# Two units' value bounds from sums of magnitudes on ScalarE instead of maxima on VectorE, with a new order of steps

## The chip, the cores and the metric

The kernel runs on one core of a Trainium2 chip. The metric is the device time of one execution in microseconds; the median of several runs is compared. Engines are named as in the profile: PE (TensorE, matmuls), PEld (TensorE's weight loads), DVE (VectorE), ACT (ScalarE), POOL (GpSimd), SP (SyncE, which issues the DMAs).

## The reference

Banded attention over 8 heads feeds a two-layer network. Heads 0 to 3 see the last 32 keys, heads 4 to 7 every fourth key of the last 128.

```python
def _attn_ref(q, k, v):                       # (8, 8, 576, 64)
    scores = scale * np.matmul(q, k.transpose(0, 1, 3, 2))
    scores = np.where(masks[None, :, :, :], scores, -1000000000.0)
    scores = scores - np.max(scores, axis=-1, keepdims=True)
    attn = np.exp(scores)
    attn = attn / (np.sum(attn, axis=-1, keepdims=True) + 1e-09)
    return np.matmul(attn, v)

def _moe_ref(x, w_in, w_out):                 # (4608, 512), (512, 2048), (2048, 512)
    h = x @ w_in
    sp = np.where(h > 20.0, h, np.log1p(np.exp(np.minimum(h, 20.0))))
    g = h * np.tanh(sp)
    return g @ w_out
```

## The kernel before

The work is cut into 16 units of 288 tokens (half of a batch entry each), numbered from 0. A unit's attention runs head by head; its output x is split into a high and a low float16 word, and so are the weights, so that each product of the network is three float16 matmuls.

The first four units are *direct*: their scores are float32 matmuls on the loaded q and k. Units from 4 on split q, k and v into words as well. The weights arrive as 64-bit numbers, 1 MB at a time, in four raw buffers, and are turned into words by VectorE, ScalarE and GpSimd during the first 180 us. This preparation shares the first units' time with their attention.

Every scale by which a split is made is a power of two taken from a bound on the values. For a direct unit `prep(u)` (line 477) takes that bound from v alone: `amax` (line 309) reduces the magnitudes of `vn` (128 partitions of 768 numbers) and `vdn` (72 or 104 partitions of 1024) to a maximum per partition on VectorE, one operation takes the greater of the two, `over_partitions` (line 317) carries it over the partitions with a transpose and a matmul on TensorE, and `pow2_scales` makes the scale `f`. With it `values` forms the divisor `den`, and `ff_scales` the factors of the network.

The order of all this is written out. `ORDER` (line 37) is a list of step names, and a loop at the end calls each step up to its next `yield` whenever its name comes up; each engine works through its instructions in the order that this leaves. A name's parts are numbers of unit, head, pair, weight matrix or column block:

- `ld`, `lv` load q and k, or v; `pr` is `prep`; `sp` a pair of heads' scores, `sc` the maxima of a head's scores, `ex` its exponentials, `tp` their transpose, `va` the products with v, `tx` the transpose of x and its split.
- `wl`, `wm`, `ws`, `ww`, `wp` load, scan, scale and split weights: matrix 0 or 1 (w_in, w_out), column block, half. `wp0.3.0` is the split of the first half of block 3 of w_in.
- `ff` is one of 16 column tiles of the first product (line 860, 12 matmuls) with its activation on ScalarE (line 865) out of one of four PSUM banks; `gt` the split of four activated tiles; `fo` the second product (line 911) and its output.
- `ol` (`open_late`, line 696) gives the raw buffers' space to new buffers and fills those with zeros on GpSimd; `mr` makes a mask.
- `kwN` gives N matmuls of zeros by zeros into an unused place (`keep_warm`, line 937): they stand where TensorE would have nothing to do.

SP issues the DMAs in this order too: a load into a raw buffer waits until the split of the weights that were in it is done, and the loads behind it wait with it.

Of the kernel before, what the change touches and what calls it, by code (L numbers as in the profile page):

```python
# [42 lines left out]
ws0.0 va0.7 tp0.4 fs0.3 wm0.2.0 tp0.5 ws0.0 tx0.0 kw2 va0.4 tx0.0 ww0.0.0 tp0.5 kw9 tx0.0 tx0.0 kw2 sp0.1 wp0.0.1
va0.5 ld1 sc0.2 va0.5 va0.4 va0.4 kw15 ex0.2 sc0.3 ex0.2 fs0.0 wm0.1.0 kw11 ex0.3 va0.5 tp0.2 wp0.0.1 ex0.3 tp0.2 kw14
tp0.3 tx0.3 pr1 tp0.3 wl0.2.1 kw2 va0.2 tx0.3 va0.3 tx0.2 lv2 va0.2 kw2 tx0.3 va0.3 tx0.2 va0.2 ww0.1.0 tx0.3 va0.3
ww0.2.0 kw16 kw16 kw2 tx0.1 tx0.2 ww0.1.0 tx0.1 tx0.2 kw11 tx0.1 kw2 sp1.0 tx0.1 wp0.0.0 ff0.12 sc1.0 sc1.1 ex1.0
sp1.1 wp0.0.0 ex1.1 ff0.15 sc1.3 wm0.2.1 wl0.1.1 ld2 ff0.14 sc1.2 ex1.3 ff0.12 ww0.2.1 tp1.0 tp1.1 ww0.2.0 ff0.13
# [5 lines left out]
ff0.8 tx1.1 fs0.1 va1.5 tp1.6 tx1.1 ff0.4 va1.5 tp1.7 tx1.1 tp1.6 ff0.11 pr2 va1.6 ff0.10 tx1.2 va1.7 tx1.2 ff0.7
va1.7 va1.6 ff0.9 va1.6 tx1.2 wm1.3.1 pr2 ff0.5 va1.7 pr2 tx1.2 tx1.3 ww1.3.0 ff0.4 ff0.6 tx1.3 ww1.3.1 gt0.0 gt0.2
pr2 tx1.3 pr2 sp2.0 ff0.5 ws1.3 ff0.6 sc2.1 tx1.3 sc2.0 ff0.7 gt0.2 ff1.8 ex2.1 ws1.3 ff1.11 ex2.0 ww1.3.1 ff1.0 gt0.1
tp2.0 sp2.1 tp2.0 fs1 ff1.10 gt0.1 ld3 ff1.8 lv3 ww1.3.0 sp2.3 ff1.0 ff1.2 ff1.11 ff1.10 wm1.1.0 sc2.2 ff1.9 wp1.3.0
ww1.1.0 ff1.4 sc2.3 ff1.2 wp1.3.0 ff1.9 ff1.6 ff1.4 wm1.1.1 ww1.1.0 wl1.2.1 ff1.1 ff1.6 ex2.2 ff1.3 sc2.7 sc2.6
fo0.3.0 wp1.3.1 ww1.1.1 ww1.1.1 ws1.1 ex2.3 wp1.3.1 ex2.6 fo0.3.1 ws1.1 wl1.2.0 gt1.2 sp3.2 wp1.1.0 gt1.2 ff1.5 sc3.4
sc3.5 gt1.2 tp2.1 fo0.3.2 fs2 tp2.1 ex3.4 va2.0 wp1.1.1 fo0.3.3 ff1.1 wp1.1.1 sp3.1 va2.0 ff1.5 ff1.12 sc3.3 wp1.1.0
ff1.3 fo0.3.3 va2.0 ff1.14 wp1.1.1 pr3 wl1.0.1 ff1.12 wp1.1.1 tp2.2 ff1.14 va2.1 ff1.7 wm1.2.0 sc3.2 wm1.2.1 ww1.2.0  # L60
ff1.13 wl1.0.0 tp2.2 ww1.2.1 tp2.3 ff1.15 ww1.2.1 tp2.3 gt1.0 va2.2 fo0.1.0 ff1.7 ww1.2.0 va2.2 gt1.1 ws1.2 gt1.0
ff1.15 ff1.13 va2.1 gt1.1 wm1.0.1 fo0.1.1 va2.1 va2.2 gt1.3 ws1.2 va2.3 fo0.1.2 wm1.0.0 gt1.3 sp3.0 va2.3 ex2.7
ww1.0.1 gt1.1 fo1.3.0 sc3.0 va2.3 tx2.0 fo1.1.0 tx2.0 wp1.2.0 tp2.6 sc3.1 wp1.2.0 fo1.3.1 tp2.6 ex3.5 tx2.0 tp2.7
va2.6 gt1.3 tp2.7 sp2.2 va2.6 wp1.2.0 tx2.1 sc2.4 ld4 fo1.3.2 ex3.0 sc2.5 wp1.2.0 tx2.1 va2.6 ex2.4 fo0.1.3 fo0.3.3
va2.7 fo1.3.3 va2.7 ex2.5 va2.7 ww1.0.1 fo1.1.1 ww1.0.0 tx2.1 tp2.5 tx2.1 fo0.2.0 tp2.5 pr4 tp2.4 tx2.3 ws1.0 ww1.0.0
tx2.3 tp2.4 fo0.1.3 wp1.2.1 va2.4 ws1.0 fo0.1.3 fo1.2.0 ex3.2 va2.4 tx2.3 va2.5 fo1.1.2 va2.5 va2.4 pr4 fo0.2.1
wp1.0.0 wp1.2.1 tp3.4 pr3 tp3.4 fo1.1.3 va2.5 tp3.5 wp1.0.1 tx2.2 tp3.5 fo1.2.1 fo1.3.3 pr3 wp1.0.1 ex3.3 fo1.3.3
# [148 lines left out]
@with_exitstack
def attn_mish_ffn_kernel(
# [91 lines left out]
    def amax(o, i, axes=None):  # L309
        axes = axes or {2: AX.X, 3: AX.XY, 4: AX.XYZ}[len(i.shape)]  # L310
        nc.vector.tensor_reduce(o, i, axis=axes, op=ALU.max, apply_absolute_value=True)
# [684 lines left out]
```

## Time and profile before

| | us |
|---|---|
| median of 3 runs | 926.02 (925.3 to 926.18) |
| the profiled execution | 926.27 |
| its span, first to last instruction | 924.2 |

The page gives each engine's busy time and its share of the span. A row of instructions reads: line, engine, operation, output<-input, count, then busy time and mean duration, then the idle time of the engine just ahead of it and what ended that. A row of a timeline begins with the start and the duration in us. A row of waits reads: engine and line that waited, what it waited for, total us, how often, the longest. A row of windows reads: stretch, its length, busy time and count, granted clock as a share, busy share of the DMA engines, GB/s.

### The profile page before, as it was taken

Reading aid. Unit: us, or ns where it says so; the run is one execution under the profiler, and the core shown is the slowest. Engines: PE = TensorE matmul, PEld = TensorE weight load, DVE = VectorE, ACT = ScalarE, POOL = GpSimd, SP = SyncE. Lnnn points to the kernel's source line nnn. Section 1 sums busy time; section 2 is a strip of 40 time slices with the busy share of each in tenths; the row PEclk is TensorE's granted clock in tenths of the full one; section 3 lists DMA queues with packets and bytes.
Section 4 is the critical chain, followed back from the end, with each engine's and each line's share of the span. In section 5 each row is a group of like instructions: output and inputs, shape, how many; then the busy total and the mean of one; then the engine's idle time right before and its main releaser. Section 6 shows DMA issues by size and latency. Waiting matters only on the chain.

```text
span 924.2 us, 22677 instructions
## 1 busy us (share of the span) xinstructions
PE 913.6 (99%) x9431; PEld 738.4 (80%) x9431; DVE 647.2 (70%) x1344; ACT 551.7 (60%) x1058; POOL 57.1 (6%) x116
## 2 busy tenths in 40 slices
PE   9999999999999999999999999999999999999998
PEld 8878778787778787878788788878787887887876
DVE  4998988677774786879888777887874775624120
ACT  3688784567465657577576565747555673635241
POOL 1002143501000000000000000000000000000000
PEclk9999999999999999999999999999999999999999
DMA  7846532130523425253726242333314221221200
GB/s 245 234 145 209 142 111 66 59 102 2 127 55 75 73 77 114 57 141 42 167 50 144 40 120 56 100 91 93 92 34 112 72 55 34 55 55 25 70 1 26
DMA packets 158102, 82.42 MB, mean 89 GB/s; under 512 B 124496, under 2 KB 153904, under 8 KB 158000
## 3 DMA queue, kind: packets, MB, share of 16 engines
q1 hardware_dynamic: 158000, 80.97, 35.1%
q8 instruction: 74, 1.21, 0.6%
q14 instruction: 28, 0.23, 0.1%
HBM read 49.02 MB, written 9.44 MB: 63 GB/s over the span
## 4 chain that ended last, share of the span: by engine, by line
PE 97%; DMA 1%; ACT 1%; DVE 1%; issue 0%; ACTq 0%; SPq 0%
PE f L860 41%; PE f L911 40%; PE psc L619 4%; PE pav L761 3%; PE f L939 3%; PE pav L755 2%; PE ptp L734 1%; PE psc L668 1%; PE psc L616 1%; DMA g<-p 0%; DMA pT<-p 0%; PE pm L369 0%; PE px L804 0%; PE pm L372 0%; DVE fo L917 0%; PE px L817 0%
## 5 line engine op out<-in xcount | busy, mean ns | idle before, releaser
L860 PE MATMUL f<-x,w 128*128 128x288 f16 x3072 | 393.6, 286 | 1.6 <-ACT hm L865 1.6
L911 PE MATMUL f<-g,w 128*128 128x288 f16 x3072 | 389.9, 286 | 0.0
L860 PEld LDWEIGHTS <-w 128*128 128x128 f16 x3072 | 294.7, 98 | 76.1 <-issue 1.7
L911 PEld LDWEIGHTS <-w 128*128 128x128 f16 x3072 | 296.4, 98 | 73.6
L865 ACT ACTIVATE hm<-f,fs 128x288 f32<-128x288 f32 x256 | 121.3, 497 | 120.9 <-PE f L860 120.2
L901 DVE SCALAR_TENSOR_TENSOR g<-hm,sg,g 128x1152 f16<-128x1152 f32 x59 | 82.9, 1411 | 55.9 <-ACT g L899 55.8
L923 ACT ACTIVATE y<-f,fo 128x288 f32<-128x288 f32 x60 | 41.8, 717 | 82.5 <-PE f L911 68.5
L899 ACT ACTIVATE g<-hm,sg 128x1152 f16<-128x1152 f32 x59 | 73.6, 1252 | 0.6
L776 DVE RECIPROCAL rec<-den 72x4 f32<-72x4 f32 (+1 forms) x128 | 21.4, 167 | 68.6 <-ACT den L772 59.9
L653 DVE TENSOR_TENSOR sb<-sb,nm 96x256 f32<-96x256 f32 (+4 forms) x120 | 55.5, 462 | 4.1
L778 DVE TENSOR_TENSOR xs<-pav,rec 72x256 f32<-72x256 f32 (+1 forms) x128 | 49.6, 387 | 11.0 <-DVE rec L776 0.5
L651 DVE TENSOR_REDUCE nm<-sb 96x2 f32<-96x256 f32 (+4 forms) x120 | 53.7, 448 | 3.3
L687 ACT ACTIVATE sb<-sb,ln_p 96x352 f32<-96x352 f32 (+3 forms) x96 | 52.8, 585 | 0.1
L772 ACT ACTIVATE den<-pav 96x3 f32<-96x3 f32 (+1 forms) x96 | 15.0, 165 | 58.7 <-PE pav L761 58.4
L645 DVE SCALAR_TENSOR_TENSOR sb<-psc,sc,m_s 72x288 f32<-72x288 f32 (+1 forms) x48 | 27.6, 575 | 27.3 <-PE psc L619 27.2
L725 DVE TENSOR_TENSOR p<-sb,p 96x352 f16<-96x352 f32 (+3 forms) x57 | 29.3, 523 | 22.1 <-ACT p L723 22.1
L534 ACT ACTIVATE q<-qn,s 128x144 f16<-128x144 f32 (+1 forms) x60 | 30.6, 590 | 10.3 <-DVE s L307 7.6
L793 ACT CAST g<-xs 96x384 f16<-96x384 f32 (+1 forms) x48 | 26.7, 562 | 14.8 <-DVE xs L778 13.1
L645 DVE SCALAR_TENSOR_TENSOR sb<-psc,sc,m_r 96x352 f32<-96x352 f32 (+1 forms) x48 | 28.4, 592 | 9.7 <-PE psc L619 9.7
L939 PE MATMUL f<-zeros 128*128 128x128 f16 x491 | 33.6, 227 | 1.0 <-DVE zeros L935 1.0
L619 PEld LDWEIGHTS <-q 64*72 64x72 f16 (+1 forms) x1008 | 26.4, 115 | 10.3 <-issue 9.5
L619 PE MATMUL psc<-k,q 64*96 64x128 f16 (+3 forms) x1008 | 32.7, 210 | 0.0
(140 smaller groups left out, 921.0 us busy)
## 6 DMA issues: line engine op xcount, KB each, us to landing
qn<-in_qT SPq DMA_DIRECT2D x16, 576.0 KB
out_T<-y SPq DMA_DIRECT2D x64, 144.0 KB
raw<-in_w_in SPq DMA_DIRECT2D x16, 512.0 KB
raw<-in_w_out SPq DMA_DIRECT2D x16, 512.0 KB
vn<-in_v SPq DMA_DIRECT2D x48, 128.0 KB
vdn<-in_vd SPq DMA_DIRECT2D x32, 104.0 KB
knd<-in_kdT SPq DMA_DIRECT2D x16, 208.0 KB
knp<-in_kT SPq DMA_DIRECT2D x8, 320.0 KB
```

The lines of the kernel that those rows point to most:

```text
L619: nc.tensor.matmul(o, q, k, start=start, stop=stop, skip_group_check=True)
L645: nc.vector.scalar_tensor_tensor(shaped(sb), shaped(pt), d["sc"][:nq], mask, ALU.mult, ALU.add)
L651: nc.vector.tensor_reduce(nm[:nq, j:j + n], x, axis=AX.X, op=ALU.max, negate=True)
L653: nc.vector.tensor_tensor(o, x, nm[:nq, j:j + n].unsqueeze(2).broadcast_to([nq, n, w]), op=ALU.add)
L687: nc.scalar.activation(x, x, AF.Exp, bias=ln_p[:nq])
L778: nc.vector.tensor_tensor(xs[:nq, :nb, (head % 2) * D:(head % 2 + 1) * D], avv[:, :, :D], rc.unsqueeze(2).broadcast_to([nq, nb, D]), op=AL ...
L860: nc.tensor.matmul(ph[:, :HT], w1[j][:, c, wi, k * P:(k + 1) * P], x_of(d, xi, c), start=(n == 0), stop=(n == len(seq) - 1))
L865: nc.scalar.activation(d["m"][j][:, k], ph[:, :HT], AF.Mish, scale=d["fs"][:, j:j + 1])
L899: nc.scalar.activation(g[:, 0], m, AF.Identity, scale=sg)
L901: nc.vector.scalar_tensor_tensor(g[:, 1], m, sg, g[:, 0], ALU.mult, ALU.subtract)
L911: nc.tensor.matmul(po[:, :HT], w2[:, e, j, wi, k * P:(k + 1) * P], d["g"][j][:, gi, k, :], start=(j == 0 and n == 0), stop=(j == NCH - 1 a ...
L939: nc.tensor.matmul(fbs[3][:, 512 - P:], zeros, zeros, start=True, stop=True)
```

## The change

For units 0 and 1 (`SUMMED`) the bound is no longer the greatest magnitude of a partition but the sum of its magnitudes, which is never less. ScalarE makes it: two passes with the function Abs, whose results are added up into `m` as they go by. The passes' own output is bfloat16 and is thrown away; it goes to the last block of `w2`, which is written with weights later. The greater of the two is then taken on VectorE as before, after a new `yield`, so `pr0` and `pr1` come up once more in the list. The list itself is new from its 39th step on.

```diff
@@ ORDER, 2682 steps before and 2690 now
-kw16 ... sp0.0 wp0.3.0 sp0.3 sc0.0 sc0.1 wp0.3.1 ex0.0 sc0.6
-ex0.1 sc0.7 ex0.0 ex0.6 wp0.3.1 ex0.1 ex0.7 ex0.6 tp0.0 pr0 wl0.2.0 sp0.2 tp0.0 ex0.7 sc0.5 kw16 kw2 pr0 sc0.4 wm0.0.1
+kw16 ... sp0.0 wp0.3.0 sp0.3 sc0.0 sc0.1 wp0.3.1 ex0.0 sc0.7
+ex0.1 sc0.6 ex0.0 ex0.7 wp0.3.0 ex0.1 ex0.6 pr0 sp0.2 wp0.3.1 sc0.4 wl0.2.0 ex0.6 pr0 sc0.5 wl0.1.0 ex0.7 kw16 kw6 pr0
...
-fo0.2.3 ff2.12 mr ol pr4 fo1.0.1 pr4 fo1.2.3 tp3.1 va3.0 pr4 fo1.2.3 ff2.0 pr4
+pr4 va3.5 ff2.12 fo1.2.3 fo0.2.3 va3.5 wp1.0.1 fo1.0.0 pr4 ff2.12 wp1.0.1 pr4 fo1.0.1 tp3.1 tp3.2 va3.0 pr4 va3.1 mr
+ol ff2.0 va3.0 pr4
...
@@ -209,6 +209,8 @@
 PE_SUBTRACTS = {0}
+
+SUMMED = {0, 1}
@@ -487,8 +489,15 @@
             vn, vdn = d["vn"], d["vdn"]
-            amax(m[:, 0:1], vn)
-            amax(m[:kd, 1:2], vdn[:kd])
+            if u in SUMMED:
+                junk = w2[:, NEC - 1, NCH - 1].rearrange("p a n -> p (a n)").bitcast(BF16)
+                for n, x, o in ((P, vn, m[:, 0:1]), (kd, vdn[:kd], m[:kd, 1:2])):
+                    nc.scalar.activation(junk[:n, :x.shape[1] * 4 * D].rearrange("p (j h d) -> p j h d", h=4, d=D), x,
+                                         AF.Abs, accum_out=o)
+                yield
+            else:
+                amax(m[:, 0:1], vn)
+                amax(m[:kd, 1:2], vdn[:kd])
             nc.vector.tensor_tensor(m[:kd, 0:1], m[:kd, 0:1], m[:kd, 1:2], op=ALU.max)
```

In the lines on `pr4`, the three that follow each other around `fo1.0.0` in the new list are the transpose of unit 4's bounds, the small diagonal matrix `dg` on VectorE, and the matmul with it; in the old list they stand behind `ol`, behind `fo1.0.1` and behind `va3.0`.

Lines behind the change carry higher numbers after it: 651 becomes 660, 420 becomes 422. VectorE's queue at unit 0's first bound, before (`nm` are negated score maxima, `w_102` is block 3 of w_in, `m` the bound):

```order
L651 TENSOR_REDUCE nm<-psc 72x4 x2
L420 SCALAR_TENSOR_TENSOR w_102<-raw,ws_405,w_102 128x2x512
L311 TENSOR_REDUCE m<-vn 128x1
L311 TENSOR_REDUCE m<-vdn 72x1
L492 TENSOR_TENSOR m<-m 72x1
L651 TENSOR_REDUCE nm<-psc 72x4 x2
L323 TENSOR_REDUCE c<-pm 1x1
L420 SCALAR_TENSOR_TENSOR w_102<-raw,ws_405,w_102 128x2x512
```

The same place on VectorE now:

```order
L660 TENSOR_REDUCE nm<-psc 72x4 x2
L422 SCALAR_TENSOR_TENSOR w_102<-raw,ws_405,w_102 128x2x512 x2
L660 TENSOR_REDUCE nm<-psc 72x4
L501 TENSOR_TENSOR m<-m 72x1
L660 TENSOR_REDUCE nm<-psc 72x4
L325 TENSOR_REDUCE c<-pm 1x1
```

The two long reductions are gone, and the second split of weights stands right behind the first. ScalarE's queue at the same place, before (line 674 are exponentials, 743 copies of their transposes, 358 the pass of `w_max`):

```order
L416 ACTIVATE w_102<-raw,ws_405 128x2x512 x2
L674 ACTIVATE sb<-psc 96x352 x2
L674 ACTIVATE sb<-psc 72x288
L743 COPY pp<-ptp 96x96
L743 COPY pp<-ptp 128x192
L674 ACTIVATE sb<-psc 72x288
L358 ACTIVATE w_99<-raw 128x1024
```

And now:

```order
L418 ACTIVATE w_102<-raw,ws_405 128x2x512 x2
L683 ACTIVATE sb<-psc 96x352 x2
L495 ACTIVATE w_103,m<-vn 128x768
L495 ACTIVATE w_103,m<-vdn 72x1024
L683 ACTIVATE sb<-psc 72x288 x2
L360 ACTIVATE w_99<-raw 128x1024
```

The two new passes stand ahead of the exponentials of two heads and of the pass of `w_max`. In the built order ScalarE loads its function tables 36 times before and after. TensorE's queue at unit 2's first scores (`sp2.0`: `psc`), before, where `px` is the last of unit 1's x:

```order
L817 LDWEIGHTS minus
L817 MATMUL px<-x,minus 128x288
L616 LDWEIGHTS ident_b
L616 MATMUL psc<-m_fb,ident_b 96x352
L619 MATMUL psc<-knp,qn 96x128 x4
```

And now, the first row being the last of 35 matmuls of zeros:

```order
L948 MATMUL f_111<-zeros 128x128
L813 MATMUL px<-ident,xs 128x72 x4
L625 LDWEIGHTS ident_b
L625 MATMUL psc<-m_fb,ident_b 96x352
L628 MATMUL psc<-knp,qn 96x128 x4
```

Before, a whole x was done and other work stood ahead of it; now the zeros and one of x's transposes stand right ahead of the scores, and 23 more zeros follow among the rows behind them. TensorE's matmuls other than those of zeros are the same in number and kind.

More of the change, by code (lines that the diff above doesn't have):

```diff
@@ L43 @@
[L43 to L47, printed above, removed]
@@ L53 @@
[L53 to L57, printed above, removed]
@@ L58 @@
[L58 to L67, printed above, removed]
@@ new lines @@
+ex0.4 pr0 wm0.0.1 pr0 ex0.5 pr0 ex0.4 tp0.0 ex0.5 ww0.0.1 kw5 tp0.1 tp0.0 ww0.0.1 tp0.1 kw12 va0.0 va0.0 kw2 tp0.6
+va0.1 tp0.6 va0.1 kw2 tp0.7 wm0.0.0 va0.0 va0.1 kw14 va0.6 tp0.7 ww0.0.0 va0.6 kw4 va0.7 va0.6 tp0.5 va0.7 ws0.0 tp0.5
+va0.7 fs0.3 tp0.4 sp0.1 ws0.0 tp0.4 wm0.2.0 sc0.2 ld1 kw4 tx0.0 kw2 va0.4 tx0.0 sc0.3 ex0.2 wp0.0.1 lv1 ww0.0.0 tx0.0
+ex0.3 tx0.0 ex0.2 ex0.3 kw16 kw2 va0.5 wp0.0.1 va0.4 wm0.1.0 kw2 tp0.2 tx0.3 va0.4 wl0.2.1 va0.5 tx0.3 ww0.1.0 kw16
+tp0.3 va0.5 tp0.2 ww0.1.0 tp0.3 kw16 va0.2 wp0.0.0 kw2 va0.3 tx0.3 va0.2 va0.3 tx0.3 va0.2 ww0.2.0 kw16 kw16 kw1 tx0.2
@@ new lines @@
+va0.3 tx0.2 wp0.0.0 kw11 tx0.1 tx0.1 kw3 tx0.2 tx0.2 ww0.2.0 kw7 tx0.1 wl0.1.1 sp1.0 tx0.1 pr1 ff0.12 sc1.0 sp1.1
+sc1.1 ex1.0 ff0.0 fs0.0 ld2 ex1.1 pr1 sc1.3 wm0.2.1 tp1.1 tp1.0 sc1.2 ff0.2 ex1.3 ww0.2.1 ff0.0 pr1 ww0.2.1 ws0.2
+ff0.12 ff0.14 tp1.1 ff0.2 ws0.2 wm0.1.1 ff0.1 pr1 tp1.0 ww0.1.1 wp0.2.1 pr1 sp1.3 pr1 ff0.14 ff0.15 wp0.2.1 wp0.2.0
+sc1.7 ff0.13 ff0.1 sc1.6 ff0.15 sp1.2 ff0.13 wp0.2.0 ex1.2 ws0.1 sc1.4 wl1.3.0 ff0.8 ex1.7 lv2 ws0.1 gt0.3 sc1.5 kw5
+va1.0 va1.1 va1.0 fs0.1 va1.1 kw7 tp1.2 wp0.1.0 va1.0 ff0.11 fs0.2 va1.1 tp1.2 fs1 ex1.4 kw4 va1.2 wp0.1.0 ex1.6 tp1.3
@@ new lines @@
+tp1.4 va1.2 tp1.3 tp1.4 va1.2 kw11 va1.3 wl1.3.1 ex1.5 ww0.1.1 ff0.3 va1.3 wl1.1.0 ff0.8 tp1.5 tx1.0 kw2 va1.4 tp1.5
+va1.3 ff0.10 wp0.1.1 gt0.3 va1.4 tp1.6 ff0.11 wp0.1.1 va1.5 ff0.3 ff0.9 va1.5 gt0.0 va1.4 wl1.1.1 va1.5 ff0.4 ff0.10
+gt0.0 tx1.0 tx1.0 ff0.4 ff0.7 tx1.0 wm1.3.1 tp1.7 tx1.1 wm1.3.0 ff0.6 tp1.6 tp1.7 kw3 va1.6 tx1.1 va1.7 ff0.9 tx1.2
+tx1.1 lv3 va1.6 tx1.2 kw4 ff0.5 gt0.2 tx1.2 va1.6 va1.7 ww1.3.0 ff0.6 ff0.5 va1.7 ff0.7 pr2 gt0.0 kw16 kw16 kw3 tx1.3
+sp2.0 tx1.3 tx1.2 kw1 tx1.3 sc2.1 tx1.3 kw11 pr2 ww1.3.1 ex2.1 kw11 ff1.8 sc2.0 gt0.2 ff1.11 gt0.1 pr2 ww1.3.1 ws1.3
@@ new lines @@
+wm1.1.0 ex2.0 ff1.10 gt0.1 ff1.8 tp2.0 ww1.1.0 tp2.1 pr2 ff1.0 ws1.3 tp2.0 ff1.11 ff1.10 ff1.4 pr2 tp2.1 wm1.1.1
+ww1.3.0 ff1.9 wp1.3.1 sp2.1 ff1.4 ww1.1.0 ff1.6 ff1.0 ld3 ff1.9 wp1.3.0 ff1.2 sc2.2 ff1.6 sc2.3 sp2.3 ex2.2 ww1.1.1
+ff1.1 sc2.7 wp1.3.0 ex2.3 ws1.1 ex2.7 sc2.6 wl1.2.0 gt1.2 ww1.1.1 ff1.5 ex2.6 wp1.3.1 fo0.3.0 ff1.2 fs2 wl1.2.1 ws1.1
+sp3.2 ff1.5 va2.0 gt1.2 fo0.3.1 va2.0 ff1.1 wp1.1.0 wp1.1.1 fo0.3.2 sc3.5 fo0.3.3 sc3.4 wm1.2.0 va2.0 tp2.2 pr3 gt1.2
+ex3.4 ff1.3 ff1.7 wp1.1.0 fo0.3.3 va2.1 tp2.2 sp3.1 va2.1 ff1.3 va2.1 va2.2 wl1.0.1 ff1.12 sc3.3 ff1.7 wp1.1.1 gt1.1
@@ new lines @@
+ff1.13 gt1.0 ff1.14 gt1.1 wm1.2.1 gt1.0 fo0.1.0 ff1.12 ff1.13 ww1.2.1 ff1.15 wp1.1.1 sc3.2 ff1.14 fo1.3.0 ww1.2.1
+wm1.0.1 va2.2 fo0.1.1 ff1.15 ww1.2.0 tp2.3 va2.2 fo1.1.0 gt1.1 tp2.7 tx2.0 tp2.7 ws1.2 tp2.3 wp1.1.1 tx2.0 gt1.3 tx2.0
+sp3.0 ex3.3 ws1.2 wl1.0.0 va2.3 fo0.1.2 sc3.0 wp1.2.1 fo1.1.1 sc3.1 va2.3 sp2.2 va2.3 ex3.1 gt1.3 tp2.6 ld4 fo1.3.1
+tp2.6 sc2.5 sc2.4 va2.6 fo1.1.2 ww1.2.0 ex2.4 gt1.3 ex2.5 va2.7 fo1.3.2 va2.7 va2.6 wm1.0.0 fo0.1.3 wp1.2.0 va2.6
+tp2.4 wp1.2.0 fo1.1.3 pr4 fo1.3.3 va2.7 wp1.2.0 ww1.0.1 tp2.5 ww1.0.0 tp2.4 tx2.3 tx2.1 tx2.3 fo0.1.3 wp1.2.0 ws1.0
@@ new lines @@
+tp2.5 fo0.1.3 tx2.3 ex3.5 fo0.3.3 tx2.1 wp1.2.1 pr3 va2.4 fo0.2.0 va2.4 pr3 va2.4 fo1.2.0 ww1.0.0 ws1.0 tx2.1 pr3
+fo1.2.1 tx2.1 ex3.0 pr3 tp3.4 va2.5 fo0.2.1 wp1.0.0 va2.5 fo1.3.3 tp3.4 va2.5 tp3.5 fo1.1.3 wp1.0.0 sp3.3 va3.4 lv4
+fo0.2.2 va3.4 sc3.6 wp1.0.0 ww1.0.1 fo1.2.2 tp3.5 fo1.3.3 va3.4 fo1.1.3 fo1.2.3 sc3.7 pr4 wp1.0.0 ex3.7 fo0.2.3 tx2.2
+pr4 tp3.0 tx2.2 fo0.0.0 wp1.0.1 tp3.0 ex3.6 va3.5 pr4 tx2.2 tp3.1 tx2.2 fo0.0.1 fo0.2.3 fo1.2.3 wp1.0.1 ex3.2 va3.0
+pr4 va3.5 ff2.12 fo1.2.3 fo0.2.3 va3.5 wp1.0.1 fo1.0.0 pr4 ff2.12 wp1.0.1 pr4 fo1.0.1 tp3.1 tp3.2 va3.0 pr4 va3.1 mr
```

252 lines of the change are left out of this document (121 added, 131 removed).

## Prediction

> **What bounds the kernel now.** I read the page's engine shares first, then the waits of TensorE (PE), then the early stretches by engine.
>
> ```profile
> span 924.2 us, 22677 instructions
> PE 913.6 (99%) x9431; PEld 738.4 (80%) x9431; DVE 647.2 (70%) x1344; ACT 551.7 (60%) x1058; POOL 57.1 (6%) x116
> ...
> L860 PE MATMUL f<-x,w 128*128 128x288 f16 x3072 | 393.6, 286 | 1.6 <-ACT hm L865 1.6
> L911 PE MATMUL f<-g,w 128*128 128x288 f16 x3072 | 389.9, 286 | 0.0
> ...
> L939 PE MATMUL f<-zeros 128*128 128x128 f16 x491 | 33.6, 227 | 1.0 <-DVE zeros L935 1.0
> ```
>
> TensorE is busy 99% of the span, so nothing counts that does not change what TensorE does or waits for. But 491 of its matmuls multiply zeros (line 939, the `kw` steps): they stand where TensorE would otherwise wait for data. So the span is an identity: **useful matmuls + zero matmuls + open waits**. The change leaves the useful ones alone. Two rows give a zero matmul's price, and one view the open waits:
>
> ```profile
> 27.63 1.84 PE L939 MATMUL f<-zeros 128*128 128x128 f16 x30
> 29.31 0.67 PE L755 MATMUL pav<-vn,pp 128*96 128x65 f32 x6
> ```
>
> From start to start, 30 of them took 29.31 − 27.63 = 1.68 us: 56 ns each (the 227 ns of the page hold the pipeline's latency).
>
> ```profile
> PE f L860 <- ACT hm L865: 1.6, 1, 1.6
> PE pm L329 <- DVE fo L917: 1.5, 1, 1.5
> PE f L939 <- DVE zeros L935: 1.0, 1, 1.0
> PE psc L616 <- ACT pp L743: 0.7, 1, 0.7
> PE pav L761 <- DMA pT<-p: 0.5, 1, 0.5
> PE pav L761 <- DMA g<-p: 0.3, 1, 0.3
> PE pav L755 <- ACT pp L743: 0.2, 1, 0.2
> ```
>
> The 1.0 us is the very start and stays. The others sum to **4.8 us**: all that a better order can win without taking zero matmuls out. VectorE (DVE) and ScalarE (ACT) in the stage that the change touches:
>
> ```profile
> core 0: us, DVE busy (x), PEclk, DMA share, GB/s
> 20.00:60.00 40.00, 38.01 (x78) 1.00 0.81 239
> 60.00:100.00 40.00, 33.98 (x85) 1.00 0.39 128
> ...
> core 0: us, ACT busy (x), PEclk, DMA share, GB/s
> 20.00:60.00 40.00, 29.15 (x59) 1.00 0.81 239
> 60.00:100.00 40.00, 34.36 (x68) 1.00 0.39 128
> ```
>
> From 20 to 60 us VectorE is 95% busy and ScalarE 73%; from 60 to 100 us it is 85% and 86%. The granted clock is 1.00 throughout, so I price no clock change.
>
> **The move of the reductions.** It takes two reductions each from `prep(0)` and `prep(1)` off VectorE and puts two passes each on ScalarE. No row shows a pass with an added sum; the nearest read the same tiles in the same shapes (line 559, unit 4):
>
> ```profile
> L311 DVE TENSOR_REDUCE m<-vn 128x1 f32<-128x768 f32 x5 | 4.7, 940 | 0.0
> L311 DVE TENSOR_REDUCE m<-vdn 72x1 f32<-72x1024 f32 x3 | 3.6, 1205 | 0.0
> ...
> L559 ACT ACTIVATE vdh<-vdn,s 72x1024 f16<-72x1024 f32 x1 | 1.1, 1140 | 0.0
> L559 ACT ACTIVATE vh<-vn,s 128x768 f16<-128x768 f32 x1 | 0.9, 921 | 0.0
> L770 ACT ACTIVATE den<-pav,eps,f 96x3 f32<-96x3 f32 x16 | 5.6, 348 | 3.4 <-PE pav L755 3.3
> ```
>
> VectorE loses 2 × (0.94 + 1.21) = 4.3 us; ScalarE gains 2 × (0.92 + 1.14) = 4.1 us. The upper bound adds one smallest pass (0.35 us) to each for its sum: 5.5 us. The lower bound is 4.1 less the 0.1 us by which neighbours in the queue overlap, four times: 3.7. I take 4.1, the row of the same shape. The Trainium skill ("ScalarE: Activation LUTs", "Rules for kernel authors") speaks against the move: plain arithmetic belongs on VectorE, which it calls up to about 3 times faster in bf16. These are float32, and the rows differ by 2% to 6% in ScalarE's favour, so here it adds nothing to the sum.
>
> What it gains the chain of unit 0 is next to nothing:
>
> ```profile
> 23.16 0.94 DVE L311 TENSOR_REDUCE m<-vn 128x1 f32<-128x768 f32 x1
> 24.03 1.20 DVE L311 TENSOR_REDUCE m<-vdn 72x1 f32<-72x1024 f32 x1
> ...
> 26.27 1.26 DVE L420 SCALAR_TENSOR_TENSOR w<-raw,ws,w 128x1024 f16<-128x1024 f32 x1
> ...
> 22.01 1.50 ACT L674 ACTIVATE sb<-psc 96x352 f32<-96x352 f32 x3 [0.93 <-PE psc L668]
> ```
>
> Before, VectorE has the bound at 24.03 + 1.20 = 25.2. In the new order ScalarE does two exponentials (22.0 to about 22.9) and then 0.92 + 1.14: 25.0. Queued behind are the exponentials of heads 7 and 6 and the pass of `w_max` (started at 24.5 before), all about 1 us later, so VectorE, free at once, waits for them. The split of weights that ran at 26.27 moves to about 23.2, right behind its twin, and frees its raw buffer 3 us sooner for the load `wl0.1.0`; the first buffer comes 1.2 us later. SP issues both loads ahead of `ld1` and `lv1`; the DMA engines are 81% busy there and move the same bytes, so I cost this at nothing: the weight passes on ScalarE are late next. Should that cover go, one late load costs those 1.2 us. Unit 1's passes lie behind unit 0's last x words on ScalarE's queue and ahead of unit 1's exponentials; the four result banks of `ff1` carry TensorE meanwhile.
>
> **The new order of steps.** Counted in the table, zero matmuls rise from 491 to 534. Up to the first `ff0` step they fall from 449 to 440; behind it they rise from 42 to 94, and 58 of these stand around `sp2.0`, where unit 1's last x words are awaited with no `ff0` step left to fill. That is 43 × 56 ns = **+2.4 us**, on TensorE's own queue and hidden by nothing. What it can buy is the 4.8 us. Two of those waits have one look: a short VectorE operation that takes ten times its length while GpSimd (POOL) works.
>
> ```profile
> 114.24 2.22 DVE L386 TENSOR_TENSOR wf<-wf,f 128x4 f32<-128x4 f32 x1
> ...
> 114.06 2.38 POOL L896 TENSOR_TENSOR g<-hm,g 128x1152 f16<-128x1152 f32 x1
> ...
> 117.14 1.41 ACT L416 ACTIVATE raw<-raw,ws 128x512 f32<-128x512 f32 x2 [4.41 <-DVE ws L390]
> ```
>
> The 4-element operation ends with POOL's (116.46 and 116.44); ScalarE stands 4.41 us behind it, and at 120 and 122.85 us TensorE waits 0.7 + 1.6 = 2.3 us. The second:
>
> ```profile
> 178.87 2.55 DVE L326 TENSOR_SCALAR dg<-ident,c 5x5 f32<-5x5 f32 x1
> ...
> 181.22 0.18 POOL L501 MEMSET m<- 128x5 f32 x1
> ...
> 181.47 0.38 PE L329 MATMUL pm<-dg,ones 5*128 5x5 f32 x2 [1.48 <-DVE fo L917]
> ```
>
> The 5x5 operation ends (181.42) with the last of the memsets that `open_late` starts (181.40). The Trainium skill ("SBUF — State Buffer", "SBUF: two separate sides") calls the port pair of the two engines an exclusive lock held for a whole instruction; the end times agree, though the memsets are many. In the new order the step that makes `dg` stands ahead of `ol`, and two groups of 12 matmuls, not one, stand between the transpose and the matmul that needs it: the **1.5 us go**. The 2.3 us depend on whether `ws1.2` meets a POOL operation again; the new order has other steps there, and POOL's work is the same. Ends 0 and 2.3; no row decides, so I take half, 1.15. The DMA waits (0.8, unit 4) and the 0.2 I keep.
>
> **The sum** on the profiled execution: 924.2 + 2.4 − 1.5 − 1.15 = 923.95 us of span. That run took 926.27, 2.07 more than its span, and the median of the runs is 0.25 lower, so a reported time is span + 1.8: **925.8 us**, no change. The other ends: all 4.8 us gone, 924.2 + 2.4 − 4.8 = 921.8, reported 923.6, a floor; all kept, 926.6, reported 928.4.
>
> **The rivals.**
> - *The zeros stand for waits that really vanish from later:* at most 0.5 us stays open. For it: VectorE has 4.3 us less to do before unit 1's work. Against: the DMA waits of unit 4 have no new cover. 924.2 + 2.4 − 4.3 = 922.3, reported 924.1.
> - *The collision comes back* at `ws1.2` or another short step, and the 1.5 us with it: 928.4. It decides from a hold of 2 us on; the rule of the lock would have it so wherever the two meet.
> - *ScalarE becomes the bound, and it is slower.* From 60 to 100 us it has 40 − 34.4 = 5.6 us idle, and unit 1's pair takes 2.1 of that. If what is left (3.5 us) is less than its waits for other engines, TensorE waits for x words or freed banks by up to those 2.1 us, on top of all old waits: 928.7, reported 930.5. Against: from 20 to 60 us 10.8 us are idle.
> - *The relief does nothing* because VectorE then waits for ScalarE, as computed for unit 0: then the order alone counts, and the forecast stands.
>
> **How the numbers follow.** A measurement of this kernel can tell about 0.2%, 1.85 us. Forecast 0.5, with the fourth rival in it (924.2 to 927.8, open waits of 0.7 to 4.4 us); first rival 0.2; collision 0.15; ScalarE 0.15. So faster 0.2, same 0.5, slower 0.3. The range goes from the floor, 923.6, to 929.5, which takes in the collision and half of the way to ScalarE's case.
>
> **What would show it.** Right: TensorE's waits sum to some 2 us, none for `pm` behind `dg`, the L495 passes near 0.92 and 1.14 us, the first `ff0` matmul about 0.5 us earlier than 49.2 us. Wrong: waits for ScalarE between 50 and 100 us (third rival), a short VectorE operation of over 2 us ahead of an idle TensorE (second), waits under 0.7 us in all (first), or L495 passes over 1.5 us.

## The result, and the profile after

The changed kernel takes **932.48 us** (median of 4 runs, 931.6 to 932.88), the kernel before beside it 925.95 us (925.3 to 926.18). The ratio is **1.0069**, with a 95% interval from 1.0057 to 1.0081: 0.7% slower, well outside the noise and outside the predicted range. The profiled execution took 932.14 us, its span is 930.5 us, 6.3 us more than before. Lines behind the change stand 9 lower in the file: 860, 911, 923 and 939 are now 869, 920, 932 and 948.

Two lines of the changed kernel's profile page first, then the waits of TensorE (engine and line, what it waited for, total us, how often, the longest):

```profile
PE 917.6 (99%) x9474; PEld 741.6 (80%) x9474; DVE 646.9 (70%) x1340; ACT 556.0 (60%) x1066; POOL 56.4 (6%) x116
...
L948 PE MATMUL f<-zeros 128*128 128x128 f16 x534 | 37.1, 227 | 2.3 <-ACT hm L874 1.2
```

```profile
PE psc L625 <- ACT sb L690: 1.4, 1, 1.4
PE f L948 <- ACT hm L874: 1.2, 2, 0.9
PE f L948 <- DVE zeros L944: 1.0, 1, 1.0
PE psc L625 <- DVE sb L662: 1.0, 1, 1.0
PE pav L764 <- ACT pp L752: 0.6, 1, 0.6
PE f L869 <- ACT y L932: 0.5, 1, 0.5
PE pav L764 <- DVE x L830: 0.3, 1, 0.3
PE ptp L743 <- DVE rec L785: 0.2, 1, 0.2
```

The zeros are 534, as counted: +43 × 56 ns = +2.4 us. Without the start the waits sum to 5.2 us, 0.4 more than before: the old ones are gone, the 1.5 us for `pm` among them, and as much is there anew. Zeros and waits make 2.8 of the 6.3 us. Two terms are missing, and the first shows in windows of 10 us (stretch, length, busy time of PE, PEld, DVE, ACT and POOL with counts, granted clock, DMA share, GB/s):

```profile
120.00:130.00 10.00, 7.99 (x69) 6.39 (x68) 8.30 (x20) 8.03 (x14) 4.00 (x2) 0.93 0.61 204
130.00:140.00 10.00, 10.00 (x76) 7.59 (x74) 6.98 (x7) 8.61 (x13) 7.20 (x3) 0.90 0.01 3
```

The granted clock is no longer 1.00: TensorE idles for 2.0 us between 125 and 129 us, and then runs at half clock for 3.4 us. The timeline of TensorE there, in which a row of 12 such matmuls took 1.63 us elsewhere:

```profile
127.05 0.32 PE L625 MATMUL psc<-m_fb,ident_b 96*96 96x384 bf16 x1 [1.41 <-ACT sb L690]
...
128.80 1.23 PE L764 MATMUL pav<-vn,pp 128*96 128x65 f32 x6 [0.60 <-ACT pp L752]
129.82 3.45 PE L869 MATMUL f<-x,w 128*128 128x288 f16 x18
```

18 of them last 3.45 us instead of about 2.4: some 1.1 us. The 6 matmuls ahead of them run at half clock too: 1.02 us from start to start (128.80 to 129.82), where the same place takes 0.56 us at full clock (a trace in point 3). Together the half clock costs **1.5 us**. The second missing term lies behind TensorE's last matmul. The end of the kernel before, and of the changed one:

```profile
909.78 9.84 PE L911 MATMUL f<-g,w 128*128 128x288 f16 x79
...
913.78 1.30 ACT L923 ACTIVATE y<-f,fo 128x288 f32<-128x288 f32 x2 [15.85 <-PE f L911]
915.11 6.25 SPq L927 DMA_DIRECT2D out_T<-y  x4
919.71 1.29 ACT L923 ACTIVATE y<-f,fo 128x288 f32<-128x288 f32 x2 [4.62 <-PE f L911]
```

```profile
913.76 10.21 PE L920 MATMUL f<-g,w 128*128 128x288 f16 x82
...
918.13 1.31 ACT L932 ACTIVATE y<-f,fo 128x288 f32<-128x288 f32 x2 [15.40 <-PE f L920]
918.93 8.90 SPq L936 DMA_DIRECT2D out_T<-y  x4
924.05 0.77 ACT L932 ACTIVATE y<-f,fo 128x288 f32<-128x288 f32 x1 [4.62 <-PE f L920]
926.71 0.77 ACT L932 ACTIVATE y<-f,fo 128x288 f32<-128x288 f32 x1 [1.89 <-DMA out_T<-y]
```

Before, TensorE ends at 919.62 and the span 4.6 us later; now it ends at 923.97 and the span 6.5 us later: **+1.95 us**. Two results are ready at about 919.4, but the new list has the output of the second, `fo15.0.3`, behind that of `fo15.3.3` on SP's queue; there are only two buffers `y`, so the last result waits 1.89 us for the buffer that this output holds. So 2.4 + 0.4 + 1.5 + 1.95 = 6.25 of the 6.3 us are accounted for.

The new passes of ScalarE by form (shortest, median and longest ns, first and last start in us), then places of VectorE and GpSimd on their timelines, which the points below use:

```profile
L495 ACT ACTIVATE w<-vn x2: 831/834/836, 23.0 to 48.0; 128x768 bf16<-128x768 f32 x2
L495 ACT ACTIVATION_READ_ACCUMULATOR w<-vn x2: 188/190/191, 23.7 to 48.7; 128x1 f32 x2
L495 ACT ACTIVATE w<-vdn x2: 1057/1057/1057, 24.0 to 48.9; 72x1024 bf16<-72x1024 f32 x1, 104x1024 bf16<-104x1024 f32 x1
```

```profile
115.03 3.52 DVE L422 SCALAR_TENSOR_TENSOR w<-raw,ws,w 128x512 f16<-128x512 f32 x2
...
114.05 3.29 POOL L905 TENSOR_TENSOR g<-hm,g 128x1152 f16<-128x1152 f32 x1
...
126.25 1.44 DVE L501 TENSOR_TENSOR m<-m 104x1 f32<-104x1 f32 x1
...
125.78 1.89 POOL L426 TENSOR_TENSOR raw<-raw 128x1024 f32<-128x1024 f32 x1
...
185.63 0.22 DVE L328 TENSOR_SCALAR dg<-ident,c 5x5 f32<-5x5 f32 x1
...
187.94 0.95 POOL L713 MEMSET p<- 96x1024 f16 x1
```

The two pieces of a weight split (line 422) take 3.52 us beside GpSimd's subtraction of activated tiles; in the kernel before, where they were over before that subtraction began (114.06), they took 1.41:

```profile
111.04 1.41 DVE L420 SCALAR_TENSOR_TENSOR w<-raw,ws,w 128x512 f16<-128x512 f32 x2
```

The greater of two bounds, 0.15 us elsewhere, lasts to the end of another subtraction of GpSimd's (127.69 and 127.67); `dg` runs before the memsets begin.

### The profile page after: what moved, and what is told of

Same layout as the page of the kernel before. It is cut to its first block, busy times and chain, and to the rows that moved or that the text cites. A ratio compares the mean times of both kernels' runs of the same rounds, so it can differ in the third digit from the quotient of the medians.

```text
span 930.5 us, 22781 instructions
## 1 busy us (share of the span) xinstructions
PE 917.6 (99%) x9474; PEld 741.6 (80%) x9474; DVE 646.9 (70%) x1340; ACT 556.0 (60%) x1066; POOL 56.4 (6%) x116
## 4 chain that ended last, share of the span: by engine, by line
PE 95%; DVE 3%; ACT 1%; DMA 1%; issue 0%; SPq 0%; DVEq 0%; ACTq 0%
PE f L869 40%; PE f L920 39%; PE psc L628 4%; PE f L948 4%; PE pav L770 3%; PE pav L764 2%; PE ptp L743 1%; DVE w L422 1%; PE psc L677 1%; DVE nm L660 0%; PE psc L625 0%; PE pm L371 0%; DVE sb L662 0%; DMA pT<-p 0%; ACT y L932 0%
## 5 line engine op out<-in xcount | busy, mean ns | idle before, releaser
L696 ACT ACTIVATE sb<-sb,ln_p 96x384 f32<-96x384 f32 (+3 forms) x96 | 52.3, 584 | 0.1
L948 PE MATMUL f<-zeros 128*128 128x128 f16 x534 | 37.1, 227 | 2.3 <-ACT hm L874 1.2
L804 DVE TENSOR_TENSOR g<-xs,g 96x384 f16<-96x384 f32 (+1 forms) x48 | 29.4, 616 | 11.2 <-ACT g L802 11.1
L948 PEld LDWEIGHTS <-zeros 128*128 128x128 f16 x534 | 34.0, 102 | 3.8 <-issue 1.7
```

Source lines behind the costliest of these rows:

```text
L696: nc.scalar.activation(x, x, AF.Exp, bias=ln_p[:nq])
L948: nc.tensor.matmul(fbs[3][:, 512 - P:], zeros, zeros, start=True, stop=True)
```

## The experiments

The kernel before ran beside each group of runs: its medians were 925.66 to 925.95 us, and the ratios are to it. The changed kernel's is 1.0069. Where times of two traces are compared: the first useful matmul starts at 15.5 to 16.9 us, at another time in each.

**1. The tail** (`e1_tail`, the changed kernel with one step moved).

```diff
-fo15.2.3 fo15.0.3 fo15.2.3 fo15.3.1 fo15.3.2 fo15.3.3 fo15.3.3 fo15.3.3 fo15.0.3 fo15.1.3 fo15.1.3
+fo15.2.3 fo15.0.3 fo15.2.3 fo15.0.3 fo15.3.1 fo15.3.2 fo15.3.3 fo15.3.3 fo15.3.3 fo15.1.3 fo15.1.3
```

> The changed kernel with one step moved: the last fo15.0.3 (the output DMA of the third to last result) stands ahead of fo15.3.1 instead of behind the DMA of fo15.3.3. My account of the +6.3 us of span: 2.4 more zero matmuls, 0.4 more waits of TensorE, about 1.5 us of half clock at 129 to 132 us, and 2.0 us behind TensorE's last matmul, where SP's queue holds a finished result back and the last result waits for its buffer. By it this run gives 932.5 - 2.0 = 930.5 us, ratio to the kernel before 1.0049, and the span ends about 6.2 us after the first of the last 12 matmuls starts, as in the kernel before, not 8.2. The rival, that the end follows TensorE alone and the late DMAs only look late, gives 932.5 (1.0069).

Measured: 930.7 us, ratio 1.0049 (1.0036 to 1.0061): −1.8 us. The timeline of its end has the last two results together again, without a wait for a buffer:

```profile
924.83 1.29 ACT L932 ACTIVATE y<-f,fo 128x288 f32<-128x288 f32 x2 [4.62 <-PE f L920]
```

The reverse, `f_tail_before`, is the kernel before with the end of its list as in the changed kernel:

```diff
-fo15.3.0 fo15.2.3 fo15.1.3 fo15.3.1 fo15.1.3 fo15.2.3 fo15.3.2 fo15.3.3 fo15.3.3 fo15.0.3 fo15.3.3 fo15.0.3
+fo15.3.0 fo15.2.3 fo15.0.3 fo15.2.3 fo15.3.1 fo15.3.2 fo15.3.3 fo15.3.3 fo15.3.3 fo15.0.3 fo15.1.3 fo15.1.3
```

> The kernel before with nothing but the order of its last outputs as in the changed kernel: the output DMA of fo15.0.3 behind that of fo15.3.3, the result of fo15.1.3 last. If the tail costs by itself what e1_tail won, the span ends about 8 us, not 6.2, behind the start of TensorE's last 12 matmuls, and the time is 925.85 + 1.8 to 2.0 = 927.7 to 927.9 us (1.0020). If e1_tail won for another reason (what stands ahead of the tail in the changed kernel), 925.85.

Measured: 927.95 us, 1.0024 (1.0015 to 1.0033): +2.0 us, and the wait for the buffer is back:

```profile
924.17 0.77 ACT L923 ACTIVATE y<-f,fo 128x288 f32<-128x288 f32 x1 [1.85 <-DMA out_T<-y]
```

The tail costs 1.8 to 2.0 us by itself, in either kernel.

**2. The zeros around `sp2.0`** (`e1_nozero`, the changed kernel with `kw16 kw16 kw3`, `kw1`, `kw11` and `kw11` struck out there).

> The changed kernel without the 58 zero matmuls around sp2.0 (35 ahead of the x of unit 1, 23 behind it). If they stand where nothing is waited for, 58 x 56 ns = 3.25 us go: 929.25 us (1.0035). If they cover a real wait for the last x of unit 1, the time stays at 932.5 (1.0069), TensorE shows about 3.2 us of new waits between 87 and 95 us, and the granted clock may drop there. By the trace of the changed kernel the scaled x is ready on VectorE at 89.74 us and the 35 zeros end at 91.15 us, so I look for about 1.4 us of gain from them and something from the 23: 930 to 931.

Measured: 930.94 us, 1.0055 (1.0042 to 1.0067): −1.5 us of 3.25. TensorE's new wait for the scaled x takes the place of part of them:

```profile
PE px L813 <- DVE xs L787: 1.5, 1, 1.5
```

So a late x was there, and the zeros covered it. What made it late stands in two timelines of the changed kernel, VectorE's and GpSimd's. The weight pass of line 401 takes 684 ns in the median of its 16 calls:

```profile
86.59 2.54 DVE L401 TENSOR_SCALAR w<-w 128x1024 int32<-128x1024 int32 x1
...
89.32 0.42 DVE L787 TENSOR_TENSOR xs<-pav,rec 72x256 f32<-72x256 f32 x1
...
86.20 2.38 POOL L905 TENSOR_TENSOR g<-hm,g 128x1152 f16<-128x1152 f32 x1
```

It started 0.39 us behind GpSimd's subtraction and ended 0.55 us behind its end; x's division stands in the queue behind it. That GpSimd holds it is read from these times, not from a run with the subtraction elsewhere; but in `e3_late_x`, where the pass starts 1.4 us later (87.96), it takes 1.24 us and ends 0.55 us behind the subtraction again. `e3_late_x` takes that apart: besides `e1_tail`'s edit it puts the division and the divisor ahead of the two long passes, and strikes out the 35 zeros.

```diff
-ff0.5 gt0.2 tx1.2 va1.6 va1.7 ww1.3.0 ff0.6 ff0.5 va1.7 ff0.7 pr2 gt0.0 kw16 kw16 kw3 tx1.3
+ff0.5 tx1.2 va1.6 va1.7 gt0.2 va1.7 ww1.3.0 ff0.6 ff0.5 ff0.7 pr2 gt0.0 tx1.3
```

> The changed kernel with the output of fo15.0.3 earlier (as in e1_tail), and: the divisor of unit 1's last head ahead of the scaling of an activated tile on ScalarE (gt0.2 behind va1.7), its division ahead of a weight pass of 2.54 us on VectorE (ww1.3.0 behind va1.7), and the 35 zero matmuls ahead of tx1.3 out. If those zeros stand for a wait that these two long operations make, x comes 2 to 3 us sooner and 932.5 - 1.8 - 2.0 to 3.1 = 927.6 to 928.7 us, without half clock at 90 us. If the wait only moves on (to the weight words or to sp2.0), it gives what leaving zeros out gave: 929.2.

Measured: 927.08 us, 1.0015 (1.0006 to 1.0023), 0.5 us better than the theory's range. The transposes of x start at 88.16 us, 3.0 us sooner:

```profile
88.16 0.43 PE L813 MATMUL px<-ident,xs 72*128 72x72 f32 x4
...
91.52 0.27 PE L322 MATMUL pm<-ident,m 128*1 128x128 f32 x1
```

The two edits together win 5.4 of the 6.5 us between the two kernels' medians, 3.6 of them beyond `e1_tail`. But not all of the 3.6 is x: a few rows on, at the last row shown, only 2.0 us are left (93.52 in the changed kernel). `e1_nozero`, which leaves x late, is as far ahead at the next row of line 869, if each trace is counted from its first useful matmul. What `e3_late_x` wins beyond that comes later: its trace has no half clock, since its waits of 1.7 and 0.6 us fall into two steps of the grid of point 3 (2 of its 11 runs took 928.3 and 928.5 us, at a lower mean clock), and its waits at about 150 and 620 us are shorter; against that stands a new wait of 1.4 us.

**3. The half clock** (`e2_clock`, the changed kernel with zeros where TensorE idled).

```diff
-va2.1 tp2.2 sp3.1 va2.1 ff1.3 va2.1 va2.2
+va2.1 tp2.2 kw16 kw8 sp3.1 kw10 va2.1 ff1.3 va2.1 va2.2
```

> The changed kernel with 34 more zero matmuls where TensorE idles after 125 us: 24 ahead of unit 3's scores (sp3.1) and 10 behind them. Only the cover changes; ScalarE, which TensorE waits for there, has the same work. If the half clock from 128.8 to 132.2 us follows from that idling, the granted clock stays at 1.00 and about 1.2 to 1.7 us are won, less what the zeros stand too long (at most 0.4): 931.0 to 931.6 us. If the half clock has another cause, the zeros win nothing or cost up to 1.9 us: 932.5 to 934.4, and the clock still falls.

Measured: 931.53 us, 1.0063 (1.0051 to 1.0076), and the clock at 129 us is 1.00. The six matmuls ahead of line 869 at full clock:

```profile
129.37 0.72 PE L764 MATMUL pav<-vn,pp 128*96 128x65 f32 x6
```

The next row starts at 129.93. The start of `fo1.3.0` comes 1.0 us sooner than in the changed kernel, though this trace's first useful matmul starts 0.55 us later: 1.5 us won. The start of `ff2.12` is only 0.1 sooner: a wait of 1.4 us for `pm` of a weight scale is new between them, which the later pace had covered. The clock follows the idling; most of what it gives back is lost again.

The clock is also a matter of chance. In the traces its changes lie on a grid of 3.41 us (a step of it is called a cell here) that runs on whatever the kernel does: in the changed kernel it falls at 128.60, is back at 132.01 and, behind the last matmul, falls at 927.32 us, 1 and 233 steps of 3.413 us later. The same two waits of TensorE, 0.66 and 1.60 us, stand in the kernel before and in `f_tail_before`; a window of TensorE alone (busy time, clock, DMA share, GB/s) and the row of its timeline behind the second wait, the kernel before first:

```profile
120.00:125.00 5.00, 3.30 (x31) 1.00 0.01 3
...
122.85 3.10 PE L860 MATMUL f<-x,w 128*128 128x288 f16 x24 [1.60 <-ACT hm L865]
```

```profile
120.00:125.00 5.00, 2.74 (x21) 0.80 0.01 3
...
123.46 4.52 PE L860 MATMUL f<-x,w 128*128 128x288 f16 x24 [1.60 <-ACT hm L865]
```

In the first the grid cuts the idling into 1.1 and 1.2 us, and the clock stays; in the second 1.8 us fall into one cell, and the 24 matmuls behind it take 4.52 us instead of 3.10. The Trainium skill ("TensorE: Matmul & The Clock Gate", "Part 1: The HAM clock gate") calls the window free-running, 3413 ns long, and has a whole idle window as the condition; the grid agrees, the condition doesn't: 1.8 us of idling in a cell were enough in every trace here, under 1.4 us never was, and between them both happened (some 1.5 us in `e2_all` and `e1_order` were enough, 1.7 us in `e1_nozero` and `e3_late_x` were not).

**4. The order without the move** (`e1_order`, the changed kernel with the maxima back on VectorE: `SUMMED = set()`).

> The changed kernel with the new order but the maxima back on VectorE for all units (no unit in SUMMED). My account puts the loss on the order (zeros, the collision at 119 to 121 us with its half clock, the tail), so the time stays near 932.5 us (931.5 to 933.5). The rival, that the new order counts on the relief of VectorE, gives up to 4.3 us more (2 x 2.15 us of reductions, now ahead of weight words and of x): 934 to 936.8 us, with new waits of TensorE for VectorE before 95 us.

Measured: 935.32 us, 1.0108 (1.0091 to 1.0125). The rival came true: the move is worth 2.8 us in the new order. Early rows of its TensorE:

```profile
25.56 0.27 PE L322 MATMUL pm<-ident,m 128*1 128x128 f32 x1 [1.12 <-DVE m L501]
...
56.44 0.44 PE L743 MATMUL ptp<-ident,sb 96*128 96x96 f32 x3 [0.62 <-DVE sb L662]
```

There are waits for VectorE at unit 0's and unit 1's bound, and half clock behind the second: the next 12 matmuls take 3.03 us instead of 1.63. (The profiled run took 937.58 us, more than the median.) `f_late_nomove` is `e3_late_x` with `SUMMED = set()`.

> As e3_late_x (the changed kernel with the output of fo15.0.3 and unit 1's last x repaired, 927.1 us), with the maxima of units 0 and 1 back on VectorE. e1_order against the changed kernel says that the move saves 2.8 us within the new order. If that saving is VectorE's time, it stays: 927.1 + 2.8 = 929.9 us. If what e3_late_x repaired (VectorE late ahead of unit 1's last x) was what the move had helped, most of it is gone: 927 to 928.

Measured: 933.06 us, 1.0069 (1.0057 to 1.0082), 6.0 us above `e3_late_x` and above either expectation; its trace has the same early waits and two stretches of half clock, from 56.8 and from 131.9 us, where `e3_late_x` has none. So part of the 6.0 us is the clock: the one run with a mean clock of 0.998 instead of 0.996 took 930.52 us, 3.4 above `e3_late_x`. By either figure the saving stays.

**5. The move without the order** (`e1_move`: the old list, `pr0` and `pr1` twice at their first place).

> The order of the kernel before, with the sums of magnitudes on ScalarE for units 0 and 1 (pr0 and pr1 come up twice at their first place, nothing else moved). If the move alone does nothing, as the prediction had it, 926 us (925 to 927). If ScalarE's 4.2 us of new work is what is late next, 927 to 930 us, with new waits of TensorE for ScalarE in the first 100 us. If the relief of VectorE is worth something by itself, 924 to 925.

Measured: 927.04 us, 1.0012 (1.0003 to 1.0021): 1.2 us are lost. ScalarE's two passes of unit 1 stand between two copies of unit 0's probabilities, and TensorE waits for the second:

```profile
43.53 1.06 ACT L495 ACTIVATE w<-vdn 104x1024 bf16<-104x1024 f32 x1
...
44.59 0.43 ACT L752 COPY pp<-ptp 96x96 f32<-96x96 f32 x2
...
45.07 0.72 PE L764 MATMUL pav<-vn,pp 128*96 128x65 f32 x6 [1.21 <-ACT pp L752]
```

`e3_move_place` puts them behind unit 0's last x (`pr1` ahead of `wp0.0.0 ff0.12`, and the second `pr1` ahead of the third).

> As e1_move (order of the kernel before, sums on ScalarE), with unit 1's two passes later: behind unit 0's last x instead of between two copies of unit 0's probabilities, where TensorE waited 1.2 us (pav for pp at 45.07 us). If the +1.2 us of e1_move are that wait, 925.7 to 925.9 us, the same as before: VectorE's 4.3 us buy nothing there. If VectorE's relief is worth something once ScalarE is out of the way, 924 to 925. If the passes are late at any place, 926.5 to 927.5.

Measured: 929.39 us, 1.0027 (1.0017 to 1.0037), worse: the copy is no longer late, but the bound is, and TensorE stands 2.6 us for it:

```profile
PE pm L322 <- DVE m L501: 2.6, 1, 2.6
```

Of its 12 runs 4 had a mean clock of 1.000 and 926.5 to 927.7 us, 8 had 0.998 and 929.3 to 930.1. That fits the grid, but their medians lie 2.4 us apart, of which the half clock in the traced run (one of the 8) accounts for about 1.5; none of the 4 was traced.

**6. The wait of 1.5 us for `dg`**, in the kernel before. `e2_ol` moves `mr ol` behind the step that makes `dg`:

```diff
-mr ol pr4 fo1.0.1 pr4 fo1.2.3 tp3.1
+pr4 fo1.0.1 pr4 mr ol fo1.2.3 tp3.1
```

> The kernel before with one edit: open_late (and mr) behind the step of unit 4's prep that makes the 5x5 diagonal matrix dg on VectorE, instead of ahead of its transpose; maxima on VectorE, all else as before. If the memsets of open_late on GpSimd hold the 5x5 operation back, as the prediction had it, TensorE's wait of 1.5 us for pm behind dg goes and the 5x5 operation takes well under 1 us: 924.2 to 924.6 us (0.9984). If the operation meets something else of GpSimd's, or what is behind the wait is late as well, no change: 925.7.

Measured: 925.71 us, 0.9997 (0.9988 to 1.0006): nothing. The 5x5 operation takes as long as before, and GpSimd's memsets start as early (176.52 in the kernel before):

```profile
179.07 2.55 DVE L326 TENSOR_SCALAR dg<-ident,c 5x5 f32<-5x5 f32 x1
...
176.73 0.96 POOL L704 MEMSET p<- 96x1024 f16 x1
```

GpSimd's queue holds nothing else ahead of them, so a later place in the list delays nothing. `e3_dg` makes `dg` on ScalarE, for unit 4 alone:

```diff
-            nc.vector.tensor_scalar(dg[:n, :n], ident[:n, :n], c[:n], None, ALU.mult)
+            if act:
+                nc.scalar.activation(dg[:n, :n], ident[:n, :n], AF.Identity, scale=c[:n])
+            else:
+                nc.vector.tensor_scalar(dg[:n, :n], ident[:n, :n], c[:n], None, ALU.mult)
```

> The kernel before with one operation on another engine: the 5x5 matrix dg of unit 4 is made by ScalarE (Identity with a scale) instead of VectorE; open_late stays where it was. The last try (open_late later in the list) left GpSimd's memsets at 176.7 to 181.6 us, since its queue has nothing else ahead of them. If it is VectorE's operation that the memsets hold back, TensorE's wait of 1.5 us for pm goes and the time is 924.3 us (0.9984). If ScalarE's small operation is held back as well, or the next VectorE operations (fo, y) are late and TensorE waits for their bank, no change: 925.8.

Measured: 924.52 us, 0.9984 (0.9975 to 0.9992), as expected: 1.3 us won, with 0.6 us of the wait left, now for ScalarE. The memsets still run there, and VectorE's other operations beside them are not held:

```profile
180.45 0.19 DVE L920 TENSOR_SCALAR fo<-f_o,f 128x1 f32<-128x1 f32 x1
...
178.24 0.94 POOL L707 MEMSET p<- 96x1024 f16 x1
...
182.28 0.38 PE L332 MATMUL pm<-dg,ones 5*128 5x5 f32 x2 [0.60 <-ACT dg L327]
```

**7. The collision of 2.3 us**, in the kernel before (`e3_dg_gate`: `e3_dg`, and gate (1, 2) taken out of `ON_POOL`, so that ScalarE and VectorE split those four tiles).

> The kernel before with dg of unit 4 on ScalarE (as in e3_dg) and one more: the split of unit 1's third group of activated tiles on ScalarE and VectorE instead of GpSimd (gate (1, 2) out of ON_POOL). Its GpSimd subtraction of 2.38 us ends with VectorE's 4-element operation of 2.22 us at 116.4 us, behind which ScalarE stands 4.41 us and TensorE then 0.7 + 1.6 us. If that meeting is the cause, 2.0 us of VectorE's delay go and its new pass costs about 1.25 us: up to 2.3 us less than e3_dg, that is 922.0 to 924.3. If VectorE's new pass is what is late next, the same as e3_dg or more.

Measured: **922.45 us**, 0.9963 (0.9951 to 0.9975), faster than both kernels. The 4-element operation beside which GpSimd worked takes 0.16 us instead of 2.22, ScalarE waits 1.55 us for the scales instead of 4.41, and TensorE's two waits are gone; one of 0.9 us for VectorE is new at 139.7 us:

```profile
112.65 0.16 DVE L389 TENSOR_TENSOR wf<-wf,f 128x4 f32<-128x4 f32 x1
...
113.50 1.44 ACT L419 ACTIVATE raw<-raw,ws 128x512 f32<-128x512 f32 x2 [1.55 <-DVE ws L393]
```

**8. Two that failed.** `e2_lv` moves the load `lv13` of the changed kernel from ahead of `tx10.2 sp12.1` to behind the output of `fo9.3.3`.

> The changed kernel with one load moved on SP's queue: v of unit 13 (lv13, seven DMAs) behind the output of fo9.3.3, no longer ahead of two transposes of unit 10's x and four of unit 11's probabilities. TensorE of the changed kernel waits at 620 us for a bank that ScalarE empties late, since ScalarE waits for a DMA transpose; in the traces of the changed kernel and of its variants so far this was 0.5, 0.9, 1.6 and 1.7 us. If the load on SP's queue makes it late, the wait goes and 0.5 to 1.5 us are won: 931 to 932. If it is the transposes themselves, the wait stays: 932.5.

Measured: 934.8 us, 1.0105 (1.0088 to 1.0123). The wait at 620 us is gone from its trace, but a new one of 1.25 us for ScalarE (`hm`, line 874) stands at 635.7 us. The profiled run took 934.0 us; why others took up to 938.25 was not traced. `e2_all` joins `e1_tail`, `e1_nozero`, `e2_clock` and `e2_lv`.

> The changed kernel with four edits at once: the output of fo15.0.3 earlier (as in e1_tail), the 58 zero matmuls around sp2.0 out (as in e1_nozero), 34 zero matmuls in where the clock falls (e2_clock) and the load lv13 later (e2_lv). If the four effects add up, 932.5 - 1.8 - 1.5 - 1.2 - 0.8 = 927.2 us, still above the kernel before, and what is left are waits of TensorE for ScalarE and VectorE. If the edits share their gains (one wait moved into the next), 928.5 to 930.

Measured: 928.93 us, 1.0032 (1.002 to 1.0043): the gains do not add up. Its trace has the waits for x (1.5 us), for `pm` (1.4) and for `hm` (1.1), each known from one of the four, and half clock behind the first. Its two runs at a mean clock of 1.000 took 927.9 us, so some 1.0 of the 1.7 us missing from the sum goes with the half clock of the others.

## Why the prediction was wrong

- **The identity was incomplete; this step failed first.** "Useful matmuls + zero matmuls + open waits" is TensorE's time at full clock up to its last matmul. It left out what lies behind that matmul, 1.95 us more by the two ends shown, and the granted clock, 1.5 us ("I price no clock change"). Neither had a bound in the range, so that 929.5 was too low. `e1_tail` and `f_tail_before` show the first term, `e2_clock` the cause of the second.
- **The open waits were mis-sized.** Of the 4.8 us the forecast kept 2.15; the changed kernel has 5.2, 3.05 more. With 1.95 and 1.5 that is the whole way from the forecast span, 923.95 us, to 930.5.
- **"I take half, 1.15" of the 2.3 us failed.** The scales' chain at that place (in the list it is `ws1.1`) did not itself meet GpSimd, but the weight split ahead of it on VectorE did: 3.52 us instead of 1.41. So the chain was late all the same, ScalarE waited 2.83 us for the scales, and TensorE 1.4 us for ScalarE. Then `m` of line 501 took 1.44 us beside GpSimd, and the output scale `fo` behind it was late: 0.6 us more. That is 2.0 us, so 0.3 of the 2.3 were won. For the changed kernel this chain is read from its rows; in the kernel before, `e3_dg_gate` shows it by taking the subtraction away. The rival "the collision comes back" was the nearest, with 928.4; with tail and clock added it comes to 931.9.
- **The zeros: right in size, wrong in what they stand for.** +43 and 2.4 us are as counted. The prediction says that unit 1's last x words are awaited there, and took the price as the price of the order. The trace shows a collision behind it: a weight pass of 0.68 us that lasts 2.54 beside GpSimd. Going around it wins about 2 us there (`e3_late_x`).
- **"The 1.5 us go": right in the result, by luck.** The place of `dg` ahead of `ol` in the list is not what decides, as `e2_ol` shows. In the changed kernel `dg` ran at 185.63 us in 0.22 us; GpSimd's next weight split began 0.14 us later (185.77), and its memsets behind that at 187.94. That the hold on VectorE's operation cost 1.3 us is shown by `e3_dg`; that the memsets make it is read from the end times.
- **"What it gains the chain of unit 0 is next to nothing" failed for the new order.** The passes were sized well: 0.83 + 0.19 and 1.06 + 0.19 us in the changed kernel, 2.1 us a pair from start to end, 4.2 in all against 4.1. But the new order relies on the relief: without it 2.8 us are lost, and 3.4 to 6.0 once x is no longer late. In the old order the move costs 1.2 us, by ScalarE's queue, which is the third rival's mechanism at unit 1.
- **Right:** the first `ff0` matmul came at 48.58 us (0.6 us sooner; 0.5 forecast); no wait for ScalarE of any length stood between 50 and 95 us except two of the zeros' own (1.2 us). **Missed:** the DMA waits of unit 4 (0.8 us), which the forecast kept, are not in the changed kernel's trace; they came and went in the kernel before's own variants too. The open waits that belong to 924.2 to 927.8 us are 0.6 to 4.2 us, not 0.7 to 4.4; nothing hangs on it.

So the change loses 6.5 us through its order, not through its move: tail 1.8 to 2.0, the late x about 2, the rest collisions and clock.

## What to carry to other kernels

Sum a span on the busiest engine in four terms, not two: its useful work, its filler and waits, its clock, and the tail behind its last instruction, where two output buffers and the order of one DMA queue are worth 2 us. Before filler is priced, ask which wait it stands for, and look at that wait's start for a short operation that takes several times its usual length while another engine works; moving that one operation, or the one it meets, to another engine won more here than any order tried. Edits that remove waits need not add up: here a later pace had covered the next wait.
